# Two chunk transposes moved to DMA, two split products made whole, and an earlier start of a state-space and expert kernel

## The chip, the cores and the metric

The kernel runs on one core of a Trainium2 chip. Its engines are TensorE (PE, with weight loads PEld), VectorE (DVE), ScalarE (ACT), GpSimd (POOL) and SyncE (SP, which only issues transfers here). The metric is the device time of one execution in microseconds; a time is the median of several runs. All times below are microseconds unless another unit stands there.

## The reference

`x` has 2048 tokens of 1024 values in bfloat16. The result is `x + A(layernorm(x)) + B(layernorm(x))`.

```
# A: a diagonal state space, 1024 complex states
Lam_bar = exp(dt * Lam);  B_bar = ((Lam_bar - 1) / Lam)[:, None] * Bmat
Bu = einsum("bld,pd->blp", x, B_bar)
h = Lam_bar * h + Bu[:, t, :]                    # over 2048 steps
y = 2 * einsum("blp,dp->bld", h, Cmat).real + x * Dskip
# B: the two tokens of highest r = x @ w_r go through a gated expert
idx = argsort(-r)[:2];  g = silu(x_sel @ w_gate);  u = x_sel @ w_up
x + scatter(idx, ((g * u) @ w_down) * sigmoid(r[idx]))
```

## The kernel before

The tokens are cut into 16 chunks of 128 and 8 groups (frames) of two chunks. A chunk goes through these stages:

- Its rows are loaded (`x.c`, tile `xt`), the layernorm's sums are taken (`bs.c`, `bn.c` on VectorE for chunks 0 to 5, `sum.c`, `sq.c` on ScalarE for the others), ScalarE makes the reciprocal deviation (`rstd.c`, two instructions on `lv` and `rstd_all`), and `apply.c` writes the normalized chunk `xn`.
- The chunk is transposed into `xnT`. Chunks 0 to 5 go through TensorE and a PSUM bank (`Tpe.c`, L367; chunk 0 in two halves `TpeA` and `Tpe.0`, L373), and ScalarE or VectorE copies the bank out (`xnT.c`, L378, L380, L383). The others go by a transposing DMA that SP issues (`T.c`, L386).
- `Bu.f.j` (L652) multiplies group f by one of eight column blocks of B, real and imaginary part, 16 products of 256 columns in one PSUM bank out of three. For five pairs (f, j) in `HALVES` the two chunks are multiplied apart, as `Bh.f.j` and `Bu.f.j` of 16 products of 128 columns each, so that the first can run before the second chunk is there. ScalarE copies the bank out (`u.f.j`, L658).
- VectorE turns `u` into the frame of a real recurrence (`TI.c`, tiles `m` and `v`), scans it (`SC.c`, tile `gf`, L722) and turns it back (`TO.c`, tiles `hT` and `m`, L763 to L765); GpSimd makes the carry from chunk to chunk. `Y.c.q` (L839) multiplies `hT` by the loaded C, `ADD.c` adds and `out.c` stores. Chunks 0 and 1 are turned and scanned in two halves.

The tables that `TI`, `SC` and `TO` need are made at the start. The parameters are loaded into `prow`, TensorE transposes them (`pP`), VectorE makes `frq` and the angles `th` (`turns`, `whole`, `angle`), ScalarE the sine `sf`, two first columns (`first`, tile `scr`) and the cosine `cf`, after loading the table of sine functions (`trig`) and before loading the one with logarithm and exponential again (`log`). `sq1` squares the cosine on VectorE, `inv` inverts it on ScalarE, `rc`, `R0`, `R`, `tan` follow on VectorE, and `kappa` (seven small GpSimd instructions on `scr`, L565 to L571) makes the factor that `ts`, `E2c` and `E2s` need.

The order of all work is the list `ORDER`: each task there issues its instructions on its own engine, and an engine runs them in that order. A transfer holds one of eight completion counters in turn, and its issue waits for the transfer that held that counter before.

The first transfers stand ahead of the list: SP loads chunk 0 in two halves (L164), ScalarE loads one parameter row, chunks 1 and 2 (L173) and three more parameter rows (L169), and then its function table (L176). `warm` tasks are products that nobody reads; three of them (`prime`, L282) have 512 columns.

Of the kernel before, what the change touches and what calls it, by code (L numbers as in the profile page):

```python
# [25 lines left out]
B.0.0 xa x.0 x.1 B.0.1 bs.0 bn.0 nmean.0 start.0 x.3 x.2 rstd.0 bs.1 bn.1 applyA apply.0 bs.2 rstd.1 apply.1 nmr1.0 warm.0 warm.1 warm.2 warm.3 warm.4  # L26
warm.5 warm.6 warm.7 warm.8 warm.9 warm.10 warm.11 warm.12 B.1.1 warm.13 warm.14 warm.15 warm.16 warm.17 warm.18 warm.19 warm.20 warm.21 warm.22 TpeA
Tpe.0 xnT0 bn.2 bs.3 bn.3 xnT.0 pP.0 Tpe.1 xnT.1 Bh.0.0 Bu.0.0 B.1.0 B.3.0 nmean.1 nmr1.1 nmean.2 rstd.2 nmr1.2 apply.2 Tpe.2 nmr.2 rstd.3 nmean.3
pcol.0 rsum Bh.0.1 Bu.0.1 nmr.1 u.0.0 wr B.2.0 dt x.5 apply.3 Tpe.3 xnT.2 Bh.1.1 Bh.1.0 B.2.1 frq rad turns whole angle abs trig den x.4 xnT.3 Bu.1.0
Bu.1.1 B.3.1 u.0.1 sin bs.5 bn.5 first Bh.1.2 Bu.1.2 bs.4 x.6 B.4.1 cos u.1.0 u.1.1 Bu.1.3 log bn.4 nmr.3 nmr1.3 sq1.0 rstd.4 apply.4 inv.0 sq1.1 rc.0  # L30
R0.0 Bu.0.2 B.7.0 B.4.0 nmean.5 R.0 Tpe.4 u.1.2 Bu.0.3 rstd.5 apply.5 nmean.4 B.5.0 nmr.5 nmr1.5 u.1.3 Bu.0.4 inv.1 tan.0 u.0.2 Tpe.5 Bu.1.4 rc.1
tan.1 B.5.1 cs ntan.0 nmr1.4 kappa sum.6 R0.1 u.0.3 Bu.1.5 ts.0.0 ts.1.0 B.6.1 TI.0.0 nmean.6 R.1 E2c.0 x.7 u.0.4 B.6.0 B.7.1 C.0.0 cin.0.0 SC.0.0.0
ends xr.0 C.0.1 ntan.1 sq.6 u.1.4 x.8 Bu.0.5 Bu.0.6 u.1.5 xnT.4 u.0.5 Bu.0.7 Bu.1.6 sum.7 xnT.5 u.0.6 nmean.7 sq.7 Bu.1.7 nmr.0 ts.0.1 u.0.7 Bu.2.0
u.1.6 u.1.7 E2c.1 nmr.4 E2n.1 SC.0.0.1 cw.0.0 gb.0.0.0 cy.0.0 cin.1.0 gb.0.0.1 rstd.7 Bu.2.1 ts.1.1 E2s.1 TI.1.0 TI.0.4 TI.1.4 E2n.0 cin.0.4 C.1.0
SC.0.4.0 SC.0.4.1 u.2.0 u.2.1 nmr.7 E2s.0 apply.7 T.7 xr.1 Bu.2.2 Bu.2.3 Bu.2.4 u.2.2 Bu.2.5 gb.0.4.0 cw.0.4 gb.0.4.1 SC.1.0.0 cy.0.4 cin.1.4 nmr1.7
TO.0.0 u.2.3 cw.1.0 SC.1.0.1 cy.1.0 Drow rstd.6 nmr.6 apply.6 T.6 x.9 x.10 u.2.4 SC.1.4.0 cw.1.4 Bu.2.6 Bu.2.7 xnT.6 gb.1.0.1 seed.0.0 TO.0.4 seed.0.1
gb.1.0.0 Y.0.0 gb.1.4.0 u.2.5 u.2.6 SC.1.4.1 xs.0 xr.2 gb.1.4.1 xs.1 cin.2.0 cy.1.4 TI.2.0 TI.3.0 C.1.1 Y.0.1 Y.0.2 u.2.7 TO.1.0 sum.9 nmean.9
seed.1.0 xnT.7 Bu.3.0 Bu.3.1 u.3.0 Bu.3.2 sq.9 rstd.9 nmr1.9 nmr.9 TO.1.4 u.3.1 Y.1.0 Y.1.1 xm.0 cin.2.4 x.12 ADD.0.0 seed.1.1 out.0.0 apply.9 Y.0.3
SC.2.0.0 SC.2.0.1 Bu.3.3 cw.2.0 Bu.3.4 xm.1 T.9 u.3.2 Bu.3.5 ADD.1.0 cy.2.0 TI.4.0 gb.2.0.0 sum.8 out.1.0 ADD.0.1 gb.2.0.1 xs.2 nmean.8 cin.3.0 Y.1.2
Y.1.3 w.0 xm.2 sum.12 seed.2.0 nmean.12 xnT.9 SC.3.0.0 r.0 sq.8 rstd.8 nmr.8 cw.3.0 apply.8 x.11 u.3.3 u.3.4 u.3.5 SC.3.0.1 cy.3.0 cin.4.0 gb.3.0.1  # L40
TO.2.0 T.8 gb.3.0.0 ADD.1.1 out.1.1 SC.4.0.0 SC.4.0.1 out.0.1 cw.4.0 cy.4.0 cin.5.0 sq.12 Bu.3.6 Bu.3.7 rstd.12 xnT.8 Y.2.0 Bu.4.0 nmr.12 xr.3 nmr1.6
sum.11 seed.2.1 nmean.11 TO.3.0 Y.2.1 nmr1.12 ADD.2.0 u.3.6 seed.3.0 u.3.7 Y.2.2 Y.2.3 xs.3 xm.3 apply.12 Bu.4.1 gb.4.0.0 T.12 out.2.0 gb.4.0.1
seed.3.1 Y.3.0 TI.5.0 u.4.0 u.4.1 ADD.2.1 sum.10 SC.5.0.0 cw.5.0 xr.4 Bu.4.2 xs.4 Y.3.1 gb.5.0.0 u.4.2 sq.11 TO.4.0 SC.5.0.1 xr.5 Y.3.2 Y.3.3 seed.4.0
out.2.1 Bu.4.3 Bu.4.4 w.1 cy.5.0 w.2 nmean.10 sq.10 rstd.10 nmr.10 apply.10 T.10 gb.5.0.1 ADD.3.0 ADD.3.1 xnT.10 Y.4.0 Bu.4.5 rstd.11 u.4.3 Y.4.1
seed.4.1 w.3 xm.4 Bu.4.6 cin.6.0 TI.6.0 SC.6.0.0 SC.6.0.1 cw.6.0 nmr.11 ADD.4.0 apply.11 xr.6 Y.4.2 x.14 u.4.4 TO.5.0 u.4.5 gb.6.0.0 u.4.6 gb.6.0.1
nmr1.10 Bu.4.7 T.11 xnT.11 x.13 seed.5.0 seed.5.1 cy.6.0 out.3.1 TI.7.0 Y.4.3 ADD.4.1 w.4 Y.5.0 xs.5 Y.5.1 out.3.0 sum.13 u.4.7 Bu.5.0 Bu.5.1 out.4.0
xm.5 nmean.13 sq.13 xs.6 seed.6.0 cin.7.0 SC.7.0.0 SC.7.0.1 rstd.13 nmr.13 x.15 ADD.5.0 TO.6.0 gb.7.0.0 Y.5.2 Y.5.3 xr.7 Bu.5.2 gb.7.0.1 xm.6 apply.13
seed.6.1 u.5.0 Y.6.0 Y.6.1 sum.14 Bu.5.3 TI.8.0 ADD.5.1 nmean.14 sq.14 out.4.1 rstd.14 nmr.14 w.5 u.5.1 Bu.5.4 Y.6.2 out.5.0 cw.7.0 xr.9 cy.7.0
cin.8.0 SC.8.0.0 SC.8.0.1 TI.9.0 TO.7.0 u.5.2 Bu.5.5 xnT.12 cw.8.0 cy.8.0 cin.9.0 seed.7.0 Y.6.3 T.13 sum.15 xnT.13 nmean.15 sq.15 nmr1.11 ADD.6.0
# [12 lines left out]
gb.14.0.1 w.38 w.39 xr.14 seed.14.0 w.40 w.41 out.11.1 TO.14.0 guT.3 Y.13.1 Y.13.2 Y.13.3 gT.3 ADD.13.0 seed.14.1 SC.15.4.0 SC.15.4.1 ADD.13.1 mm.6
mm.7 Y.14.0 SC.15.0.0 SC.15.0.1 xr.15 rows row_.3 row_.1 row_.2 Y.14.1 Y.14.2 Y.14.3 SC.15.6.0 SC.15.6.1 ymb hotY.14.1 hotY.14.0 xs.14 seed.15.0 xm.14
TO.15.0 ADD.14.0 seed.15.1 ADD.14.1 seed.15.2 out.12.1 TO.15.4 TO.15.6 out.12.0 hotY.15.0 Y.15.0 Y.15.1 Y.15.2 Y.15.3 Y.15.4 Y.15.5 Y.15.6 Y.15.7
hotY.15.2 hotY.15.1 Y.15.8 xs.15 xm.15 ADD.15.0 ADD.15.1 ADD.15.2 out.13.0 out.13.1 fix out.14.0 out.14.1 out.15.0 out.15.1 out.15.2
# [39 lines left out]
def kernel(  # L105
# [135 lines left out]

    add(("xa",), "none", 2.85, lambda: None, key=-1)
    for c in range(NCH):
        if c < 3:
            add(("x", c), "none", (3.35, 0.6, 0.6)[c], lambda: None, [("x", c - 1)] if c else [], key=c, takes=[("xt", c, [("apply", c)])])
        elif c == 3:
            add(("x", c), "SP", 0.45, lambda c=c: load_x(c), key=-89.85, takes=[("xt", c, [("apply", c)])], mb=0.28, lag=0.2)
# [917 lines left out]
```

## Time and profile before

| | |
|---|---|
| median of 3 runs (lowest, highest) | 255.83 (255.74, 256.82) |
| profiled execution: time, span | 255.56, 253.8 |
| PE busy | 246.7 (97%) |
| DVE busy | 239.8 (94%) |
| ACT, POOL busy | 175.5 (69%), 93.1 (37%) |
| chain that ended last | PE 65%, DVE 25%, POOL 3%, ACT 2% |

The span runs from the first to the last instruction; 1.76 of the profiled time lies around it. TensorE and VectorE are both busy nearly all the time, so the chain that ended last passes from one to the other: it is mostly on VectorE, ScalarE and GpSimd up to 83 and on TensorE from there on.

### The profile page before, as it was taken

The page shows a single profiled execution, that of the slowest core. Times are in us where ns is not written, and L with a number is a line of the kernel's source. Part 1 is how long each engine was busy: PE and PEld are TensorE (multiplying, and loading weights), DVE is VectorE, ACT ScalarE, POOL GpSimd, SP SyncE. Part 2 cuts the span into 40 slices and gives each one's busy share as a digit, 9 for nine tenths or more (in the row PEclk, how much of TensorE's full clock was granted, in tenths as well). Part 3 has the DMA queues.
Part 4 walks back from the last instruction along what each step waited for, and adds up shares of the span by engine and source line. Part 5 has one row for each costly group of instructions (what it writes and reads, how often), then busy time and mean ns, then how long its engine had stood idle before and what let it go on. Part 6 is the DMA issues. An engine that isn't in the chain of part 4 may idle for free.

```text
span 253.8 us, 5220 instructions
## 1 busy us (share of the span) xinstructions
PE 246.7 (97%) x2052; PEld 167.0 (66%) x2052; DVE 239.8 (94%) x312; ACT 175.5 (69%) x302; POOL 93.1 (37%) x130
## 2 busy tenths in 40 slices
...
GB/s 196 225 228 184 191 254 274 148 134 198 99 159 45 83 89 242 40 256 228 120 89 1 105 166 69 76 3 155 321 340 381 361 316 388 384 250 357 23 68 83
DMA packets 66277, 46.50 MB, mean 183 GB/s; under 512 B 45828, under 2 KB 52362, under 8 KB 66252
## 3 DMA queue, kind: packets, MB, share of 16 engines
...
q0 software_dynamic: 112, 0.27, 0.3%
q14 instruction: 9, 0.07, 0.1%
...
## 4 chain that ended last, share of the span: by engine, by line
PE 65%; DVE 25%; POOL 3%; ACT 2%; DMA 1%; issue 1%; ACTq 0%; DVEq 0%; POOLq 0%
PE pY L839 38%; PE pB L652 22%; DVE gf L722 7%; PE pG L1043 3%; DVE v L703 3%; DVE m L702 2%; DVE m L764 1%; DVE hT L763 1%; DVE ot L850 1%; DVE hT L765 1%; PE pD L1083 1%; DMA xt<-in_A_x_dram 1%; DVE st L294 1%; DVE ts L585 1%; DVE E2c L591 1%
## 5 line engine op out<-in xcount | busy, mean ns | idle before, releaser
L652 PE MATMUL pB<-xnT,BT 128*128 128x256 bf16 (+1 forms) x1104 | 116.9, 265 | 0.6 <-ACT xnT L378 0.3
L839 PE MATMUL pY<-CT,hT 128*128 128x512 bf16 (+1 forms) x528 | 115.7, 373 | 0.2 <-DVE hT L765 0.2
L652 PEld LDWEIGHTS <-BT 128*128 128x128 bf16 x1104 | 100.9, 98 | 16.4 <-issue 1.7
L839 PEld LDWEIGHTS <-hT 128*128 128x128 bf16 x528 | 50.8, 98 | 55.4 <-issue 2.1
L738 POOL TENSOR_TENSOR cw<-gf,tL 128x16 f32<-128x16 f32 (+1 forms) x34 | 41.1, 1210 | 110.8 <-DVE gf L722 101.3
L722 DVE TENSOR_TENSOR_SCAN gf<-R,v 128x1040 f32<-128x1040 f32 (+1 forms) x34 | 68.8, 2056 | 0.5
L658 ACT CAST u<-pB 128x512 bf16<-128x512 f32 x64 | 35.7, 577 | 18.3 <-PE pB L652 15.5
L815 ACT ACTIVATE pY<-xr,nmr_all,rstd_all 128x512 f32<-128x512 bf16 (+1 forms) x33 | 24.9, 763 | 29.2 <-DVE ot L850 24.7
L728 ACT CAST gb<-gf 128x1024 bf16<-128x1024 f32 (+1 forms) x34 | 31.4, 941 | 8.0 <-DVE gf L722 8.0
L850 DVE TENSOR_TENSOR ot<-pY,ot 128x512 bf16<-128x512 f32 (+1 forms) x33 | 21.5, 663 | 3.3 <-PE pY L839 2.1
L765 DVE TENSOR_TENSOR hT<-hT,m 128x2048 bf16<-128x2048 bf16 (+2 forms) x20 | 20.2, 1012 | 0.7
L703 DVE TENSOR_TENSOR v<-u,m 128x2048 bf16<-128x2048 bf16 (+2 forms) x20 | 20.2, 1012 | 0.7
L702 DVE TENSOR_TENSOR m<-u,E1t 128x2048 bf16<-128x2048 bf16 (+2 forms) x20 | 20.1, 1005 | 0.6
L764 DVE TENSOR_TENSOR m<-gb,E2s 128x2048 bf16<-128x2048 bf16 (+2 forms) x20 | 20.3, 1014 | 0.0
L824 ACT ACTIVATE ot<-xr,nmr_all,rstd_all 128x1024 bf16<-128x1024 bf16 x16 | 19.8, 1237 | 0.6 <-DMA out_dram<-ot 0.5
L763 DVE TENSOR_TENSOR hT<-gb,E2c 128x2048 bf16<-128x2048 bf16 (+2 forms) x20 | 20.0, 1000 | 0.0
L753 POOL CAST v<-cy 128x16 bf16<-128x16 f32 (+1 forms) x17 | 12.7, 747 | 1.0
L754 POOL TENSOR_TENSOR v<-cy,v 128x16 bf16<-128x16 f32 (+1 forms) x17 | 12.5, 738 | 1.4
L334 ACT ACTIVATE xn<-xt,nmr_all,rstd_all 128x1024 bf16<-128x1024 bf16 x10 | 12.4, 1237 | 0.2
L309 ACT ACTIVATE xn<-xt,nmean_all 128x1024 bf16<-128x1024 bf16 x10 | 11.5, 1150 | 0.2
L829 DVE TENSOR_TENSOR ot<-ot,Drow 128x1024 bf16<-128x1024 bf16 x16 | 10.9, 680 | 0.0
L303 ACT ACTIVATE xn<-xt 128x1024 bf16<-128x1024 bf16 x10 | 10.5, 1050 | 0.0
...
## 6 DMA issues: line engine op xcount, KB each, us to landing
...
```

The costliest lines, as they stand in the source:

```text
L652: nc.tensor.matmul(out=pB[:, ri, ts_], lhsT=BT[ri][j][:, k, :], rhs=xnT_frame(f)[:, k, ts_], start=(k == 0), stop=(k == DT - 1))
L658: nc.scalar.copy(out=u_tiles[f][:, :, j, :], in_=pB_tiles.pop((f, j))[:])
L702: nc.vector.tensor_tensor(out=m[:, :, js, :], in0=u[:, ::-1], in1=E1t[:, :, js, :], op=ALU.mult)
L703: nc.vector.tensor_add(out=rot, in0=u, in1=m[:, :, js, :])
L722: nc.vector.tensor_tensor_scan(out=flat(gf), data0=flat(R[:, js, :]), data1=flat(v[:, ri, js, :]), initial=0.0, op0=ALU.mult, op1=ALU.add)
L728: nc.scalar.copy(out=gb_tiles[c][:, ri, js, :], in_=gf_tiles[c, js.start, ri][:, :, 2:])
L738: nc.gpsimd.tensor_tensor(out=cw_tiles[c, js.start][:, ri, :, 0:n], in0=g.unsqueeze(1).to_broadcast([128, 2, n]), in1=tL[:, ri, :, js], op ...
L764: nc.vector.tensor_tensor(out=m[:, :, js, :], in0=g[:, ::-1], in1=both(E2s, js), op=ALU.mult)
L765: nc.vector.tensor_add(out=rot, in0=rot, in1=m[:, :, js, :])
L815: nc.scalar.activation(out=pY[:, 0:d_.stop - d_.start], in_=y_tiles["xr", c][:, d_], func=ACT.Identity, bias=nmr_all[:, c:c + 1], scale=rs ...
L839: nc.tensor.matmul(out=pY, lhsT=h_tiles[c][:, ri, j, :], rhs=CT[ri][h][:, j, d0:d0 + w], start=False, stop=end, skip_group_check=True)
L850: nc.vector.tensor_add(out=ot, in0=y_tiles.pop(("pY", c, dh))[:, 0:d_.stop - d_.start], in1=ot)
```

## The change

- Chunks 4 and 5 are transposed by DMA (`PE_T` from 6 to 4): `T.4` and `T.5` on SP replace `Tpe.4`, `Tpe.5` and their copies.
- `HALVES` loses (1, 1) and (1, 2).
- ScalarE's queue issues four early transfers, three parameter rows and then chunk 1. Chunk 2 is issued by SP, the fourth parameter row by GpSimd.
- The halves of chunk 0 are transposed into two PSUM banks, chunk 1 into a bank of the ring for products; 15 `warm` tasks stand in place of 23.
- `ORDER` is another list.

```
-start and first two lines of ORDER: B.0.0 xa x.0 x.1 B.0.1 bs.0 bn.0 nmean.0 start.0 x.3 x.2 rstd.0 ...
+start.0 warm.0 ... warm.6 xa bs.0 x.0 bn.0 rstd.0 warm.7 x.1 bs.1 bn.1 warm.8 x.3 x.2 ... B.0.0 B.0.1 rstd.1 applyA apply.0 B.1.0 pP.0 TpeA
...
-    load_param(nc.scalar, 0)
-    for c in (1, 2):
-        nc.scalar.dma_start(out=xt_tiles[c][:], in_=x2[c * T:(c + 1) * T, :])
-    for i in range(1, 4):
+    for i in range(3):
         load_param(nc.scalar, i)
+    nc.scalar.dma_start(out=xt_tiles[1][:], in_=x2[T:2 * T, :])
     nc.scalar.preload_act_table_set("natural_log_exp_and_others")
...
     nc.vector.tensor_copy(out=tt[:], in_=t_i[:])
+    load_param(nc.gpsimd, 3)
...
-        pT_tiles[c] = psum.tile([128, DT, 128], BF16, name="pT", tag="misc" if odd else "T")
+        pT_tiles[c] = psum.tile([128, DT, 128], BF16, name="pT", tag="B" if c == 1 else "misc" if odd else "T", bufs=3 if c == 1 else 1)
...
-        if h == 0:
-            pT_tiles[0] = psum.tile([128, DT, 128], BF16, name="pT", tag="T")
+        pT_tiles[0, h] = psum.tile([128, DT // 2, 128], BF16, name="pT", tag="misc" if h else "T")
...
-    NWARM = 23
+    NWARM = 15
...
-    PE_T = 6
+    PE_T = 4
...
-    HALVES = ((0, 0), (0, 1), (1, 0), (1, 1), (1, 2))
+    HALVES = ((0, 0), (0, 1), (1, 0))
```

The new order moves instructions in many places; two matter below. The first is the head of SP's queue, before; `BT_0` is the first column block of B, with its real and imaginary part, and the first row is chunk 0:

```order
L164 DMA xt<-in_A_x_dram 128x512 x2
L234 DMA_TRANSPOSE BT_0_116<-in_A_B_re_dram 128x8x128
L234 DMA_TRANSPOSE BT_0_124<-in_A_B_im_dram 128x8x128
L230 DMA xt<-in_A_x_dram 128x1024
L234 DMA_TRANSPOSE BT_1_125<-in_A_B_im_dram 128x8x128
```

And the same head now:

```order
L164 DMA xt<-in_A_x_dram 128x512 x2
L229 DMA xt<-in_A_x_dram 128x1024 x2
L233 DMA_TRANSPOSE BT_0_114<-in_A_B_re_dram 128x8x128
L233 DMA_TRANSPOSE BT_0_122<-in_A_B_im_dram 128x8x128
L233 DMA_TRANSPOSE BT_1_115<-in_A_B_re_dram 128x8x128
```

Chunks 3 and 2 now stand ahead of the first two blocks of B. Further on, `T.4` stands between the blocks 5 and 6 of B and `T.5` behind block 7.

The second place is ScalarE around the sine tables, before; `xnT` rows copy a transposed chunk, `u` rows a finished product, `sf` is the sine, the two `scr` rows are `first`, `cf` is the cosine, and the table loads are `trig` and `log`:

```order
L483 ACTIVATE rad<-scr 128x8
L505 ACT_TABLE_LOAD
L380 COPY xnT<-pT 128x8x128
L658 CAST u<-pB 128x2x256
L517 ACTIVATE sf<-th 128x1024
L512 ACTIVATE scr<-th 128x8
L513 ACTIVATE scr<-cf,halfpi 128x8
L520 ACTIVATE cf<-cf,halfpi 128x1024
L658 CAST u<-pB 128x2x256 x2
L508 ACT_TABLE_LOAD
```

And now:

```order
L378 COPY xnT<-pT 128x8x128 x2
L481 ACTIVATE rad<-scr 128x8
L503 ACT_TABLE_LOAD
L510 ACTIVATE scr<-th 128x8
L511 ACTIVATE scr<-cf,halfpi 128x8
L656 CAST u<-pB 128x2x256
L515 ACTIVATE sf<-th 128x1024
L656 CAST u<-pB 128x2x256 x2
L518 ACTIVATE cf<-cf,halfpi 128x1024
L506 ACT_TABLE_LOAD
```

Both copies of transposed chunks now stand ahead of `rad` and the table, `first` ahead of the sine, and three copies of products between `first` and the cosine; before, one stood ahead of the sine and two behind the cosine.

## Rows read from the trace of the kernel before

**Rows 1.** ScalarE's timeline at the start: start, duration, instruction, [idle before <-releaser]

```profile
0.73 0.59 ACTq L169 DMA_DIRECT2D prow<-in_A_Lambda_re_dram  x1
...
2.63 0.30 ACTq L169 DMA_DIRECT2D prow<-in_A_log_dt_dram  x1
...
4.86 1.28 ACT L176 ACT_TABLE_LOAD   x1 [4.86 <-DMA xt<-in_A_x_dram]
```

**Rows 2.** Chain that ended last, one piece: start, duration, what (chunk 1's load)

```profile
1.36 3.17 DMA xt<-in_A_x_dram
```

**Rows 3.** VectorE's timeline from the first chunks to the first hT

```profile
4.78 1.23 DVE L294 BATCH_NORM_STATS2 st<-xt 128x6 f32<-128x512 bf16 x2
6.05 0.21 DVE L297 BATCH_NORM_AGGREGATE mv<-st 128x2 f32<-128x12 f32 x1
...
6.71 0.74 DVE L330 TENSOR_SCALAR xn<-xt,mv,rstd_all 128x512 bf16<-128x512 bf16 x2 [0.46 <-ACT rstd_all L263]
...
10.86 0.21 DVE L297 BATCH_NORM_AGGREGATE mv<-st 128x2 f32<-128x12 f32 x1
...
12.63 1.23 DVE L493 TENSOR_TENSOR th<-frq,tt 128x1024 f32<-128x1024 f32 x1
...
15.88 0.69 DVE L501 TENSOR_SCALAR cf<-th 128x1024 int32<-128x1024 int32 x1
...
20.20 0.64 DVE L524 TENSOR_TENSOR th<-cf 128x512 f32<-128x512 f32 x1
...
22.58 0.69 DVE L534 TENSOR_TENSOR gf<-gf,cf 128x512 f32<-128x512 f32 x1
...
29.48 1.31 DVE L585 TENSOR_TENSOR ts<-sf,scr 128x512 f32<-128x512 f32 x2 [0.46 <-POOL scr L571]
...
53.77 0.70 DVE L765 TENSOR_TENSOR hT<-hT,m 128x1024 bf16<-128x1024 bf16 x1
```

**Rows 4.** TensorE's timeline up to 84

```profile
3.04 1.49 PE L282 MATMUL prime<-ident 128*128 128x512 bf16 x3
4.32 1.86 PE L399 MATMUL warm<-ident 128*128 128x128 bf16 x24
...
11.54 0.62 PE L367 MATMUL pT<-ident,xn 128*128 128x128 bf16 x8
11.99 1.95 PE L652 MATMUL pB<-xnT,BT 128*128 128x128 bf16 x32
...
27.47 26.36 PE L652 MATMUL pB<-xnT,BT 128*128 128x256 bf16 x240
53.67 5.36 PE L839 MATMUL pY<-CT,hT 128*128 128x512 bf16 x24
...
83.26 1.90 PE L839 MATMUL pY<-CT,hT 128*128 128x512 bf16 x8 [0.23 <-DVE hT L765]
```

**Rows 5.** ScalarE's timeline around the sine tables

```profile
16.01 1.07 ACT L517 ACTIVATE sf<-th 128x1024 f32<-128x1024 f32 x1
...
17.41 1.15 ACT L520 ACTIVATE cf<-cf,halfpi 128x1024 f32<-128x1024 f32 x1
18.47 1.05 ACT L658 CAST u<-pB 128x512 bf16<-128x512 f32 x2
19.54 1.28 ACT L508 ACT_TABLE_LOAD   x1
...
21.27 0.62 ACT L530 ACTIVATE gf<-th 128x512 f32<-128x512 f32 x1
```

**Rows 6.** GpSimd's timeline, first and last instruction of kappa

```profile
24.77 0.50 POOL L565 TENSOR_TENSOR scr<-scr,rad 128x16 f32<-128x16 f32 x1
...
29.17 0.28 POOL L571 TENSOR_SCALAR scr<-scr 128x16 f32<-128x16 f32 x1
```

**Rows 7.** DMA issues: transfer, queue, kind, count, median time to landing

```profile
BT<-in_A_B_re_dram SPq DMA_TRANSPOSE x8, 4.3
```

**Rows 8.** SP's timeline, two blocks of B: start, time to issue

```profile
22.62 2.67 SPq L234 DMA_TRANSPOSE BT<-in_A_B_im_dram  x2
```

More of the change, by code (lines that the diff above doesn't have):

```diff
@@ L25 @@
 ORDER = """
[L26 to L49, printed above, removed]
@@ L62 @@
[L62 to L65, printed above, removed]
+start.0 warm.0 warm.1 warm.2 warm.3 warm.4 warm.5 warm.6 xa bs.0 x.0 bn.0 rstd.0 warm.7 x.1 bs.1 bn.1 warm.8 x.3 x.2 warm.9 warm.10 warm.11 warm.12
@@ new lines @@
+warm.13 warm.14 B.0.0 B.0.1 rstd.1 applyA apply.0 B.1.0 pP.0 TpeA Tpe.0 bs.3 apply.1 Tpe.1 xnT0 xnT.0 Bh.0.0 xnT.1 Bu.0.0 nmean.0 B.1.1 nmr1.0 nmr.0
+bn.3 rstd.3 B.2.0 bs.2 nmean.1 bn.2 rstd.2 nmean.3 nmr1.3 pcol.0 dt wr apply.3 Tpe.3 apply.2 Tpe.2 Bh.0.1 Bu.0.1 u.0.0 x.4 frq rsum x.5 xnT.3 xnT.2
+Bh.1.0 Bu.1.0 Bu.1.1 B.2.1 turns whole angle abs rad trig first u.0.1 Bu.0.2 bs.4 bs.5 sin u.1.0 u.1.1 den nmr1.1 nmean.2 nmr1.2 bn.5 cos bn.4 log
+nmean.4 sq1.0 sq1.1 inv.0 rc.0 R0.0 B.3.0 nmean.5 Bu.1.2 B.3.1 Bu.1.3 u.0.2 rstd.4 apply.4 u.1.2 nmr.1 inv.1 nmr.2 u.1.3 R.0 x.6 tan.0 B.4.0 rstd.5
@@ new lines @@
+Bu.0.3 ntan.0 nmr1.4 u.0.3 rc.1 tan.1 cs ntan.1 B.4.1 Bu.1.4 B.5.0 B.5.1 nmr.4 kappa ts.0.1 u.1.4 ts.1.0 TI.0.0 apply.5 Bu.0.4 Bu.0.5 T.4 Bu.1.5 B.6.0
+sum.6 B.6.1 u.0.4 Bu.0.6 u.0.5 E2c.1 B.7.0 nmean.6 nmr.3 sq.6 Bu.1.6 u.1.5 ts.0.0 B.7.1 Bu.0.7 R0.1 T.5 rstd.6 nmr1.6 E2c.0 R.1 x.7 cin.0.0 E2n.0
+u.0.6 xnT.4 E2n.1 xnT.5 TI.1.0 u.1.6 nmr.6 u.0.7 SC.0.0.0 SC.0.0.1 xr.0 sum.7 nmr.5 nmean.7 Bu.1.7 Bu.2.0 sq.7 rstd.7 C.1.0 ends C.0.0 u.1.7 Bu.2.1
+Bu.2.2 gb.0.0.1 gb.0.0.0 TI.0.4 cin.0.4 ts.1.1 TI.1.4 SC.0.4.0 u.2.0 u.2.1 SC.0.4.1 gb.0.4.0 gb.0.4.1 cw.0.0 cy.0.0 cin.1.0 nmr.7 C.0.1 Bu.2.3 u.2.2
```

71 lines of the change are left out of this document (45 added, 26 removed).

## The prediction

> **What bounds the kernel now.** I read the page's busy shares first: TensorE 97% and VectorE 94% of a span of 253.8, in an execution of 255.56. Two engines that full bound each other, so a part of the sum must name which one waits. The timelines answer that. TensorE runs without a gap from the transpose at 11.54 to the first output product at 53.67 and on to 83.26, where it waits 0.23 for `hT` of VectorE [rows 4]. VectorE has its last `hT` half for the first output products done at 53.77 + 0.70 = 54.47 [rows 3], 0.8 after those products began: they read the first half of the states first, so nothing was lost. VectorE is thus as late as it may be, with nothing to spare, and its own chain starts at the first layernorms and runs through the sine tables of ScalarE and `kappa` of GpSimd [rows 3, 5, 6]. An edit that frees TensorE alone gains only what VectorE can follow.
>
> **The start.** ScalarE's table load began at 4.86, after a sixth issue had waited for chunk 1 to land [rows 1, 2], and VectorE waited 0.46 for the deviation it delayed, to apply chunk 0 at 6.71 [rows 3]. With four issues and no wait the table is in long before. But in VectorE's order chunk 1's statistics stand ahead of that apply; they took from 4.78 to 6.05 + 0.21 = 6.26 [rows 3]. So the gain is at most 6.71 - 6.26 = 0.45. Chunk 1 is now ScalarE's fourth issue: 0.73 + 0.59, then two short ones like the one of 0.30 [rows 1], so about 2.05 in place of 1.36. It landed 3.17 after its issue [rows 2]; the same again is 5.2, and since less stands in its queue I take 5.0. VectorE then starts these statistics 0.2 later than at 4.78, and applies chunk 0 at about 6.45: a gain of 0.25. The other end is the 4.3 that a block of B of the same 256 KB took to land [rows 7]: 2.05 + 4.3 = 6.35, apply at 7.85, a loss of 1.1.
>
> The Trainium skill bears on this place (DMA: Bandwidth & Descriptors, section Issuing engines are not separate DMA queues): transfers of all issuing engines interleave on the same 16 DMA engines, so that another queue saves issuing time alone. By it chunk 1 shares with chunk 3, which SP now issues early, lands at 5.2 or later, and the gain falls to 0.05; were queues apart it would be the full 0.45. Chunk 1's 3.17, beside other loads, is on the rule's side, but no row shows a queue alone.
>
> **TensorE.** A transpose of a chunk takes 11.99 - 11.54 = 0.45 from start to start [rows 4]; two go: 0.9. A whole product takes 16 x (53.67 - 27.47) / 240 = 1.75; the same in two halves took 1.95 at most, with the modelled end of the last [rows 4]. So each of two costs 0 to 0.2 less; I take 0.05 each. Together 1.0 less. Against that, chunks 3 and 2 are now transposed ahead of the second column block, behind both chunks' statistics: these ended at 10.86 + 0.21 [rows 3], then two casts and apply 3, together 0.8, so 11.9 less the 0.25 gained, or 0.1 later than 11.54. And `Bu.0.3` takes the PSUM bank whose copy `u.0.2` now stands behind the inverse: by the ScalarE times below that copy ends at 23.75 where TensorE would be at 23.4, 0.35. TensorE could be at the first output products at 53.67 - 1.0 + 0.1 + 0.35 = 53.1.
>
> **The table chain, without the 0.25.** VectorE's work up to the angles is the same set, so `th` starts at 12.63 again and the absolute value ends at 15.88 + 0.69 = 16.57 [rows 3]. ScalarE's `first` waits for that and now stands ahead of the sine, and three product copies stand between it and the cosine. Sine and `first` took 17.41 - 16.01 = 1.40, the cosine 18.47 - 17.41 = 1.06, two copies 1.05 [rows 5]. So the cosine ends at 16.6 + 1.40 + 3 x 0.53 + 1.06 = 20.65, where it ended at 18.47. The squares, at 20.20 before [rows 3], wait for it; that alone is 0.5. The table load takes 1.3 and the inverse 22.58 - 21.27 = 1.3 [rows 3, 5]: `rc.0` comes at 23.25 in place of 22.58. Before it VectorE had also applied chunk 4, about 0.5, which now comes later, so VectorE is 1.1 behind. Next on ScalarE are `u.0.2` and the deviation of chunk 4, 0.5 each; with 0.8 for two GpSimd instructions `kappa` starts at 25.0, takes 29.17 + 0.28 - 24.77 = 4.7 [rows 6] and ends at 29.7. VectorE's `ts`, which waited 0.46 for it and began at 29.48 [rows 3], begins at 29.7 with two instructions still to do that were done before (apply 5 and a part of R, 1.2 together). From there to the last `hT` it needed 54.47 - 29.48 = 25.0; these two come on top and one half scan falls behind it, which I set equal: 54.7. Less 0.25: 54.45.
>
> **The sum.** Of the two halves of chunk 0's states the first is now turned back last, and the first output product reads it: TensorE, ready at 53.1, starts at 54.45, 0.8 later than at 53.67. Behind this point its work is the same, and the new order leaves VectorE as little room as the old one, so I leave its later waits as they were. The execution takes 255.56 + 0.8 = 256.35. The median of the runs lies 0.27 above the profiled execution; by it the same sum is 256.6, and I forecast 256.5.
>
> Cost nothing: the two ScalarE copies (2 us that nobody waited for after 30), the separate PSUM banks (the copy no longer waits for VectorE's, but the products still need both), the parameter row on GpSimd (TensorE's `pP` now stands ahead of chunk 0's transposes and waits for it; GpSimd issues it near 1.6, and a landing after 4.3 [rows 7] is before 6.45; later than that it delays all), fewer `warm` tasks.
>
> **Rivals.**
>
> 1. VectorE follows, and TensorE's time counts. For it: 1.0 less work is certain, and ScalarE loses two copies. Against it: the cosine cannot start before the copies ahead of it. TensorE at 53.1 in place of 53.67: 255.0, by the median 255.25, and 254.9 if the bank's 0.35 goes too. Chance 0.22.
>
> 2. Slower: chunk 1 lands late. Everything on VectorE stands behind its statistics, and VectorE is the bound up to the output products, so each 0.1 is paid in full. It decides from a landing of about 5.5, where 0.8 has become 1.3; at 6.35 the time is 256.35 + 1.35 = 257.7, by the median 258.0. For it: issued 0.7 later, beside chunks 3 and 2; against it: chunk 1 is alone in its queue. Chance 0.20.
>
> 3. SP stands still at `T.4` until chunk 4 is applied, near 25.1, with the blocks 6 and 7 of B behind. At 1.33 an issue [rows 8] the last is issued at 25.1 + 4 x 1.33 = 30.4 and lands 4.3 later, 34.7 [rows 7]; TensorE wants it ten products before 53.1, at 35.6. A stop 0.9 longer delays TensorE, one 2.2 longer the whole. With 3 longer it is 257.4. Chance 0.06.
>
> 4. TensorE's clock. The three 512-column products took (4.32 - 3.04) / 3 = 0.43 each [rows 4], the 1.2 GHz level; later 128 columns take 0.061 at most, the 2.4 GHz one. Eight `warm` tasks less leave TensorE idle from about 5.2 to 6.45, and little used up to the first products. At the low level 32 products cost 0.107 in place of about 0.056 each, 1.6 in all; TensorE is then at 54.7 and the end 0.3 to 0.8 later: 257. Chance 0.07. The Trainium skill has this as a rule (TensorE: Matmul & The Clock Gate, section What's actually happening): activity releases the throttle and an idle stretch brings it back; the granted clock on the page is full in all 40 slices, so no row of before shows a fall.
>
> **How the numbers follow.** The forecast has 0.45. About 0.5% (1.3) is what a measurement of this kernel tells from no change: faster means under 254.55, slower over 257.1. Faster: half of rival 1 with a luckier start, 0.12. Slower: nearly all of rivals 2 and 3, half of 4, a little of the forecast, 0.31. The same: the rest, 0.57. The range runs from rival 1's early end, 254.6, to rival 2's price, 258.0; the forecast alone has 255.9 to 257.1.
>
> **What would show it.** On VectorE, chunk 0's apply near 6.45 and chunk 1's statistics ending just before; idle time ahead of the squares (0.5 or more), ahead of `rc.0` (about 1.0) and ahead of `ts` (0.5 to 1.0, released by GpSimd); on ScalarE the cosine ending near 20.4; on TensorE a wait of about 1.3 for `hT` at the first output products, near 54.4. If TensorE starts them near 53.1 without a wait, the chain was mis-sized and rival 1 holds. If VectorE waits for a load ahead of chunk 1's statistics until after 5.5, it is rival 2.

## The result and the profile after

| | before | after |
|---|---|---|
| median (lowest, highest), 10 runs each | 255.86 (255.34, 256.82) | 257.83 (256.83, 258.90) |
| profiled execution: time, span | 255.56, 253.8 | 257.90, 256.1 |
| PE busy, DVE busy | 246.7, 239.8 | 245.6, 239.8 |
| first output product | 53.67 | 55.75 |
| from there to the end of the span | 200.1 | 200.4 |

The ratio of the changed kernel's time to that of the kernel before is 1.0069, 95% interval [1.0046, 1.0092]: 1.8 slower. The forecast was 256.5 with a range of 254.6 to 258.0. The traces differ by 2.3, and 2.08 of it has arisen when TensorE starts the first output products; what follows takes the same time in both within 0.3. So the place to look is the first 56.

ScalarE's timeline at the start (start, duration, instruction), where the third row is chunk 1's load:

```profile
0.74 0.59 ACTq L169 DMA_DIRECT2D prow<-in_A_Lambda_re_dram  x1
...
2.03 0.39 ACTq L173 DMA_DIRECT2D xt<-in_A_x_dram  x1
2.45 1.28 ACT L174 ACT_TABLE_LOAD   x1 [2.45 <-issue]
```

The chain of waits holds that load:

```profile
2.03 4.63 DMA xt<-in_A_x_dram
```

The table is in 2.4 earlier than before [rows 1], as forecast. But chunk 1 took 4.63 from its issue to landing, at 6.66, where it took 3.17 [rows 2]. VectorE's timeline (in brackets: idle time before, and who ended it) shows what that does:

```profile
3.04 1.29 DVE L293 BATCH_NORM_STATS2 st<-xt 128x6 f32<-128x512 bf16 x2 [0.44 <-DMA xt<-in_A_x_dram]
...
6.69 1.29 DVE L293 BATCH_NORM_STATS2 st<-xt 128x6 f32<-128x512 bf16 x2 [2.12 <-DMA xt<-in_A_x_dram]
...
8.13 0.68 DVE L329 TENSOR_SCALAR xn<-xt,mv,rstd_all 128x512 bf16<-128x512 bf16 x2
...
14.09 1.22 DVE L491 TENSOR_TENSOR th<-frq,tt 128x1024 f32<-128x1024 f32 x1
...
22.39 1.29 DVE L522 TENSOR_TENSOR th<-cf 128x512 f32<-128x512 f32 x2 [0.66 <-ACT cf L518]
25.00 0.69 DVE L532 TENSOR_TENSOR gf<-gf,cf 128x512 f32<-128x512 f32 x1 [1.31 <-ACT gf L529]
...
31.31 1.29 DVE L583 TENSOR_TENSOR ts<-sf,scr 128x512 f32<-128x512 f32 x2 [0.63 <-POOL scr L569]
...
55.00 0.69 DVE L763 TENSOR_TENSOR hT<-hT,m 128x1024 bf16<-128x1024 bf16 x1
```

The first two rows are the statistics of chunk 0 and of chunk 1. VectorE stood idle for 2.12 and applied chunk 0 at 8.13, 1.42 later than at 6.71 [rows 3]. The angles are 1.46 later, `rc.0` 2.42, the last half of `hT` 1.22. TensorE's timeline:

```profile
5.10 0.18 PE L465 MATMUL pP<-ident,prow 32*128 32x32 bf16 x1 [0.21 <-DMA prow<-in_B_w_r_dram]
8.55 1.03 PE L371 MATMUL pT<-ident,xn 128*128 128x128 bf16 x8 [3.27 <-DVE xn L329]
9.93 1.03 PE L366 MATMUL pT<-ident,xn 128*128 128x128 bf16 x8 [0.34 <-DVE xn L322]
10.75 3.62 PE L650 MATMUL pB<-xnT,BT 128*128 128x128 bf16 x32
14.16 1.20 PE L366 MATMUL pT<-ident,xn 128*128 128x128 bf16 x16
15.20 40.42 PE L650 MATMUL pB<-xnT,BT 128*128 128x128 bf16 x400
55.75 4.49 PE L837 MATMUL pY<-CT,hT 128*128 128x512 bf16 x19
```

TensorE idled 3.27 before chunk 0 came. Then 32 products of 128 columns took 3.62, where 1.95 had done [rows 4]. Busy times and granted clock by stretch (the last three figures are the clock, 1.00 being full speed, the busy share of the DMA engines, and GB/s) say why:

```profile
5.00:10.00 5.00, 1.29 (x10) 0.94 (x11) 3.28 (x8) 1.22 (x4) 0.62 (x3) 0.76 1.10 227
10.00:15.00 5.00, 5.00 (x53) 5.00 (x54) 4.80 (x15) 2.60 (x8) 1.46 (x5) 0.55 0.92 225
...
9.00:11.00 2.00, 1.66 (x17) 1.40 (x15) 1.97 (x6) 0.59 (x2) 0.00 (x0) 0.50 1.01 215
...
13.00:15.00 2.00, 2.00 (x26) 2.00 (x25) 1.97 (x7) 0.69 (x3) 0.77 (x2) 0.64 1.02 257
```

The granted clock fell to half (0.50), the 1.2 GHz level, within the idle stretch and rose again before 15; in the kernel before it reads full in every slice. The DMA engines are busy nearly throughout (1.10 and 0.92). ScalarE's timeline around the sine tables:

```profile
19.09 1.05 ACT L515 ACTIVATE sf<-th 128x1024 f32<-128x1024 f32 x1
20.05 1.26 ACT L656 CAST u<-pB 128x512 bf16<-128x512 f32 x2
21.20 1.15 ACT L518 ACTIVATE cf<-cf,halfpi 128x1024 f32<-128x1024 f32 x1
22.37 1.28 ACT L506 ACT_TABLE_LOAD   x1
```

The cosine ends at 22.35, 3.8 later than before [rows 5]. The two copies ahead of it wait for TensorE's products. The chain of waits goes through them:

```profile
10.96 3.41 PE pB L650 x32
14.37 0.99 PE pT L366 x16
15.37 5.33 PE pB L650 x80
20.72 0.58 ACT u L656
21.31 1.05 ACT cf L518
```

So TensorE's slow clock reaches VectorE's tables.

### The profile page after: what moved, and what is told of

Its sections match the earlier page's. It is cut to its first block, busy times and chain, and to the rows that moved or that the text cites. A ratio compares the mean times of both kernels' runs of the same rounds, so it can differ in the third digit from the quotient of the medians.

```text
span 256.1 us, 5068 instructions
## 1 busy us (share of the span) xinstructions
PE 245.6 (96%) x1969; PEld 166.5 (65%) x1988; DVE 239.8 (94%) x312; ACT 173.5 (68%) x300; POOL 86.3 (34%) x131
## 4 chain that ended last, share of the span: by engine, by line
PE 75%; DVE 15%; DMA 3%; ACT 2%; POOL 2%; issue 2%; ACTq 0%; SPq 0%; DVEq 0%
PE pY L837 38%; PE pB L650 31%; PE pG L1041 3%; DVE gf L720 2%; DMA xt<-in_A_x_dram 2%; DVE v L701 1%; DVE hT L763 1%; DVE m L700 1%; DVE hT L761 1%; DVE m L762 1%; DVE ts L583 1%; DVE ot L848 1%; DVE gb L713 1%; DVE E2c L589 1%; DVE E2s L589 1%
## 5 line engine op out<-in xcount | busy, mean ns | idle before, releaser
L837 PE MATMUL pY<-CT,hT 128*128 128x512 bf16 (+1 forms) x509 | 112.4, 372 | 2.0 <-issue 0.6
L650 PEld LDWEIGHTS <-BT 128*128 128x128 bf16 x1072 | 102.2, 99 | 15.2 <-PE pG L1041 0.4
L736 POOL TENSOR_TENSOR cw<-gf,tL 128x16 f32<-128x16 f32 (+1 forms) x34 | 35.0, 1028 | 116.6 <-DVE gf L720 115.7
L751 POOL CAST v<-cy 128x16 bf16<-128x16 f32 (+1 forms) x17 | 13.5, 792 | 1.1
L744 POOL TENSOR_TENSOR cy<-cw 128x16 f32<-128x16 f32 (+1 forms) x17 | 11.1, 652 | 1.3
L752 POOL TENSOR_TENSOR v<-cy,v 128x16 bf16<-128x16 f32 (+1 forms) x17 | 10.2, 599 | 1.4
```

Source lines behind the costliest of these rows:

```text
L650: nc.tensor.matmul(out=pB[:, ri, ts_], lhsT=BT[ri][j][:, k, :], rhs=xnT_frame(f)[:, k, ts_], start=(k == 0), stop=(k == DT - 1))
L736: nc.gpsimd.tensor_tensor(out=cw_tiles[c, js.start][:, ri, :, 0:n], in0=g.unsqueeze(1).to_broadcast([128, 2, n]), in1=tL[:, ri, :, js], op ...
L837: nc.tensor.matmul(out=pY, lhsT=h_tiles[c][:, ri, j, :], rhs=CT[ri][h][:, j, d0:d0 + w], start=False, stop=end, skip_group_check=True)
```

## The experiments

Theory: VectorE's chain bounds up to the first output products, and chunk 1's late landing is most of its delay. Rivals: the lost clock; the order around the sine tables; the moved transposes. Medians, with the ratio to runs of the kernel before on the same chip:

| kernel | time | ratio, interval | chunk 0 applied | first output product |
|---|---|---|---|---|
| `x1_first` | 255.93 | 0.9994 [0.9967, 1.0021] | 6.77 | 53.83 |
| `warm_on` | 257.44 | 1.0051 [1.0024, 1.0078] | 8.13 | 55.18 |
| `sine_first` | 257.23 | 1.0051 [1.0022, 1.0079] | 8.61 | 55.91 |
| `three` | 255.56 | 0.9981 [0.9949, 1.0014] | 6.83 | 53.36 |
| `x23_behind` | 257.71 | 1.0070 [1.0047, 1.0094] | 9.16 | 57.00 |
| `best` | 256.09 | 1.0009 [0.9987, 1.0030] | 6.64 | 54.46 |
| `before_dma45` | 256.35 | 1.0019 [0.9998, 1.0040] | 6.65 | 57.18 |
| `before_early` | 258.63 | 1.0112 [1.0077, 1.0147] | 8.91 | 56.21 |
| `x1_sp` | 255.33 | 0.9994 [0.9979, 1.0008] | 5.75 | 52.81 |
| `best2` | 255.19 | 0.9981 [0.9967, 0.9995] | 6.11 | 52.41 |
| `x1_pe45` | 257.47 | 1.0062 [1.0046, 1.0077] | 6.77 | 55.05 |
| `before_x1sp` | 255.58 | 1.0000 [0.9975, 1.0024] | 5.81 | 55.07 |

The last two columns are of the one profiled execution, which lies well above the median in `before_dma45` (258.34, by 2.0), `x23_behind` (259.15, by 1.4), `before_x1sp` (256.74, by 1.2), `sine_first` (258.38, by 1.2) and `best` (257.02, by 0.9).

**Chunk 1 first: `x1_first`.**

```diff
+    nc.scalar.dma_start(out=xt_tiles[1][:], in_=x2[T:2 * T, :])
     for i in range(3):
         load_param(nc.scalar, i)
-    nc.scalar.dma_start(out=xt_tiles[1][:], in_=x2[T:2 * T, :])
```

> The changed kernel with chunk 1's transfer as the first issue of ScalarE's queue, ahead of the three parameter rows. Theory (chunk 1's late landing at 6.66 delays all of VectorE, and VectorE bounds the time up to the first output products): chunk 1 is issued near 0.75 and lands by 5.0, the first half of chunk 0 is applied by 6.7 in place of 8.13, the first output products start 1.1 to 1.5 earlier than at 55.75, and the time falls by as much, to 256.3 to 256.8. Rival (TensorE's lost clock sets the end, or the table chain absorbs the earlier start): apply comes earlier but the first output products move by less than 0.5 and the time stays above 257.3.

VectorE and TensorE of this kernel:

```profile
3.93 1.29 DVE L293 BATCH_NORM_STATS2 st<-xt 128x6 f32<-128x512 bf16 x2 [1.33 <-DMA xt<-in_A_x_dram]
...
6.77 0.68 DVE L329 TENSOR_SCALAR xn<-xt,mv,rstd_all 128x512 bf16<-128x512 bf16 x2
...
23.07 0.69 DVE L532 TENSOR_TENSOR gf<-gf,cf 128x512 f32<-128x512 f32 x1 [1.31 <-ACT gf L529]
...
29.39 1.29 DVE L583 TENSOR_TENSOR ts<-sf,scr 128x512 f32<-128x512 f32 x2 [0.63 <-POOL scr L569]
...
53.08 0.69 DVE L763 TENSOR_TENSOR hT<-hT,m 128x1024 bf16<-128x1024 bf16 x1
```

```profile
12.82 40.60 PE L650 MATMUL pB<-xnT,BT 128*128 128x128 bf16 x400
53.83 5.35 PE L837 MATMUL pY<-CT,hT 128*128 128x512 bf16 x23 [0.41 <-DVE hT L763]
```

Chunk 0 is applied 1.36 earlier than in the changed kernel, the first output product 1.92 earlier, and the time falls by 1.9: all of the loss, by moving one line. The theory's 1.1 to 1.5 was too small, because the granted clock stayed at full speed here too (1.00 from 5 to 15). The first row shows the price: chunk 0, on another engine's queue, now comes 0.9 later (its statistics begin at 3.93, in the changed kernel at 3.04).

**The clock: `warm_on`.** `hold` is a task list of the products of `warm`:

```diff
-B.1.0 pP.0 TpeA
+B.1.0 pP.0 hold.0 hold.1 ... hold.25 TpeA
```

> The changed kernel with 52 products of 128 columns that nobody reads, behind the transpose of the parameters on TensorE, so that it isn't idle from 5.1 to about 8.3. Theory (TensorE waits for VectorE at the first output products anyway): the granted clock stays at full speed through 7.6 to 14.5, the first products of chunk 0 take half the time, but the first output products start within 0.3 of 55.75 and the time stays at 257.5 to 258.2. Rival (the lost clock is the loss): 256.0 to 257.0.

```profile
10.00:15.00 5.00, 4.22 (x71) 3.92 (x72) 4.79 (x15) 3.55 (x9) 1.02 (x5) 1.00 1.08 212
```

```profile
8.13 0.68 DVE L330 TENSOR_SCALAR xn<-xt,mv,rstd_all 128x512 bf16<-128x512 bf16 x2
...
24.43 0.69 DVE L536 TENSOR_TENSOR gf<-gf,cf 128x512 f32<-128x512 f32 x1 [1.30 <-ACT gf L533]
```

With the clock full and chunk 0 applied at the very same 8.13, `rc.0` comes 0.57 earlier and the first output product too (55.18). The theory said at most 0.3, since TensorE would only wait; it left out that ScalarE's copies of TensorE's products stand ahead of the cosine. The medians are 0.39 apart with intervals that overlap; the 0.57 is shown by the traces alone. The clock is the lesser part. TensorE's own delay stood close behind this one: in the changed kernel its last product before that point ends at 15.20 + 40.42 = 55.62, and the last half of `hT` at 55.69.

**The order around the sine tables: `sine_first`.**

```diff
-trig first u.0.1 Bu.0.2 bs.4 bs.5 sin u.1.0 u.1.1 den nmr1.1 nmean.2 nmr1.2 bn.5 cos bn.4 log
+trig u.0.1 sin first Bu.0.2 bs.4 bs.5 den nmr1.1 nmean.2 nmr1.2 bn.5 cos u.1.0 u.1.1 bn.4 log
```

> The changed kernel with ScalarE's order around the sine tables as before: sine, then the two first columns, then the cosine, with one product copy ahead and two behind. Theory (the cosine behind three copies is the other part of VectorE's delay): the cosine ends near 20.2 in place of 22.35, the squares start without a wait, rc.0 starts near 23.7 in place of 25.0, the first output products 0.5 to 1.1 earlier; time 256.8 to 257.4. Rival (the table chain has slack, all of the loss is the late chunk): within 0.3 of the changed kernel, 257.5 to 258.1.

Here chunk 1 happened to land 0.48 later still (2.03 + 5.11 in the chain, apply at 8.61). Counted from the apply, `rc.0` comes 0.28 earlier than in the changed kernel and the first output product 0.32. The medians differ by 0.6, the ratios by 0.0018, inside their intervals. This run can't size the order by itself: counted from the apply, TensorE's long run of products also starts 0.24 earlier (15.44 in place of 15.20), and its 32 first products took 3.49 in place of 3.62: the granted clock rose at nearly the same moment (0.56 and 0.55 from 10 to 15) although chunk 0 came later. The next run sizes it with the clock at 1.00.

**All three: `three`,** the edits above together, with 12 of the 26 tasks.

> All three at once: chunk 1 first on ScalarE's queue, 24 more products that nobody reads on TensorE before chunk 0 comes, and ScalarE's order around the sine tables as before. Theory (VectorE's chain bounds; the two parts on it add): the first output products 1.6 to 2.6 earlier than at 55.75, near 53.6, and the time 255.2 to 256.2, level with the kernel before. Rival (TensorE's work bounds once VectorE is ahead, 1.0 less than before): 254.8 to 255.2. Rival (the loss lies behind the first output products): above 257.

```profile
22.59 0.69 DVE L536 TENSOR_TENSOR gf<-gf,cf 128x512 f32<-128x512 f32 x1 [1.02 <-ACT gf L533]
```

```profile
12.88 40.42 PE L654 MATMUL pB<-xnT,BT 128*128 128x128 bf16 x400
53.36 5.35 PE L841 MATMUL pY<-CT,hT 128*128 128x512 bf16 x23
```

53.36 without a wait, and 255.56: level with the kernel before, as the theory had it. Against `x1_first` the first output product gains 0.47. `rc.0` comes at 22.59 in place of 23.07, although chunk 0 is applied 0.06 later, and TensorE's long run of products starts no earlier (12.88 and 12.82). So the order around the sine tables costs about 0.5 on VectorE, the lower end of what was expected of `sine_first`; the medians, 0.37 apart, don't separate it from noise.

**Why chunk 1 was late: `x23_behind`.** SP's head is the first block of B, then chunks 3 and 2:

```diff
-x.3 x.2 ... B.0.0 B.0.1
+B.0.0 x.3 x.2 B.0.1
```

> The changed kernel with the first transposing load of B issued ahead of chunks 3 and 2 on SP instead of behind them; chunk 1 stays the fourth issue of ScalarE's queue, at 2.03. It tells why chunk 1 landed at 6.66. Theory (the transfers share the same DMA engines, and chunks 3 and 2 on SP took chunk 1's share): chunk 1 lands 3.2 to 3.6 after its issue, at 5.2 to 5.6, the first half of chunk 0 is applied by 7.2, time 256.0 to 256.7. Rival (it is the place in its own queue, or one DMA engine that is behind whatever SP issues): chunk 1 lands at 6.4 or later, apply at 7.9 to 8.3, time 257.3 to 258.1.

```profile
2.03 5.66 DMA xt<-in_A_x_dram
```

The rival's time and landing came (257.71, 7.69; the apply, 9.16, is later still), and the theory fell in this form: chunks 3 and 2 are not what chunk 1 needs to be ahead of, since with a block of B issued at 1.66 in their place the time is the same. What the two have in common is 256 KB issued before chunk 1. But this trace, of the slowest of its twelve runs, isn't a plain case of waiting in line. The trace has sixteen completion marks for each load: fourteen of chunk 1's stand by 5.73, 3.7 after its issue, the last two at 7.04 and 7.70, and the block of B issued ahead of it landed only at 7.9. In the changed kernel twelve of chunk 1's stand by 6.09 and the last at 6.67. Why single marks come late stays open. The next run puts chunk 1 ahead.

**Chunk 1 behind chunk 0 on SP: `x1_sp`.**

```diff
-    nc.scalar.dma_start(out=xt_tiles[1][:], in_=x2[T:2 * T, :])
+    nc.sync.dma_start(out=xt_tiles[1][:], in_=x2[T:2 * T, :])
```

> The changed kernel with chunk 1 issued by SP right behind the two halves of chunk 0, ahead of chunks 3 and 2, and not by ScalarE. Its issue comes at about 1.66 in place of 2.03, and all of x now stands in one queue in the order in which it is wanted. Theory (the DMA engines are busy from 2 on and move what was issued first; chunk 1 came last of the first four chunks): chunk 1 lands by 5.2, 0.5 to 1.5 before chunks 3 and 2, the second half of chunk 0 stays near 3.5, apply by 6.7, time 255.4 to 256.2. Rival (one or two DMA engines lag whatever stands ahead, as with the first block of B ahead of chunks 3 and 2): chunk 1 lands at 6 or later, apply at 7.5 or later, time above 257.

```profile
1.67 0.43 SPq L173 DMA_DIRECT2D xt<-in_A_x_dram  x1
```

```profile
2.91 1.29 DVE L293 BATCH_NORM_STATS2 st<-xt 128x6 f32<-128x512 bf16 x2 [0.32 <-DMA xt<-in_A_x_dram]
...
4.36 1.23 DVE L293 BATCH_NORM_STATS2 st<-xt 128x6 f32<-128x512 bf16 x2
...
5.75 0.68 DVE L329 TENSOR_SCALAR xn<-xt,mv,rstd_all 128x512 bf16<-128x512 bf16 x2
```

Issued 0.36 earlier and with only chunk 0 and parameter rows of 2 KB ahead, chunk 1 landed 2.4 after its issue, in place of 4.63, and VectorE didn't wait for it. Against `x1_first` the apply moves by 1.02 and the first output product by 1.02 as well: up to there each 0.1 at the start is paid, or won, in full. The times show less of it: the medians, 255.93 and 255.33, are 0.6 apart and of different chips, and the two ratios are equal.

**The early transfers in the kernel before: `before_early`,** with that part of the change alone, **and `before_x1sp`,** the same with chunk 1 on SP behind chunk 0 and chunk 2 ahead of chunk 3.

```diff
-    load_param(nc.scalar, 0)
-    for c in (1, 2):
-        nc.scalar.dma_start(out=xt_tiles[c][:], in_=x2[c * T:(c + 1) * T, :])
-    for i in range(1, 4):
+    for i in range(3):
         load_param(nc.scalar, i)
+    nc.scalar.dma_start(out=xt_tiles[1][:], in_=x2[T:2 * T, :])    # before_x1sp: nc.sync
...
+    load_param(nc.gpsimd, 3)
...
-B.0.0 xa x.0 x.1 B.0.1 ... x.3 x.2
+xa x.0 x.1 x.3 x.2 B.0.0 B.0.1
```

> The kernel before with the other part of the change: ScalarE's queue issues three parameter rows and then chunk 1, GpSimd the fourth row, SP chunks 3 and 2 ahead of the first block of B; all else as before. Theory (this part alone makes the loss): chunk 1 lands at 6.4 to 7, the first half of chunk 0 is applied at 7.9 to 8.4 in place of 6.71, the last half of hT ends 1.2 to 1.7 later than at 54.47, time 257.0 to 257.7. Rival (the loss comes from the new order of the instructions, which can't cover the late chunk): 255.8 to 256.5.

> The kernel before with the early transfers of the change, but chunk 1 issued by SP right behind chunk 0, then chunks 2 and 3, then the blocks of B; ScalarE issues three parameter rows and its table, GpSimd the fourth row. All else, the order too, as before. Theory (the early transfers are worth what they do to chunk 1's landing, in either order of the instructions): chunk 1 lands near 4.1, the first half of chunk 0 is applied at 5.6 to 6.0 in place of 6.71, the last half of hT ends 0.6 to 1.0 earlier than at 54.47; time 254.6 to 255.1. Rival (the old order can't use an earlier start, since TensorE or a later load sets it): 255.3 to 255.8.

`before_early` is 2.85 slower, more than expected and more than the whole change: chunk 1's load took 5.41, and the granted clock averaged 0.69 from 10 to 15. In `before_x1sp` chunk 0 was applied at 5.81, as expected, but the time is that of the kernel before. TensorE of it:

```profile
10.58 0.62 PE L366 MATMUL pT<-ident,xn 128*128 128x128 bf16 x8
13.39 1.96 PE L651 MATMUL pB<-xnT,BT 128*128 128x128 bf16 x32 [2.19 <-DMA BT<-in_A_B_re_dram]
```

The second column block of B, which SP issued at 7.50, came only near 13.4, and TensorE lost there what it had won. The new order transposes chunks 3 and 2 before it wants that block; in this execution the old one couldn't use the early start. Three of the twelve runs took 254.91 to 254.96, inside the expected 254.6 to 255.1, so the wait may not come in each; that is not shown, since the one trace is of a slower run.

**The moved transposes: `before_dma45`,** `T.4` and `T.5` behind `B.5.1` and two split products made whole, in the kernel before, **and `x1_pe45`,** `x1_first` with `Tpe.4` and `Tpe.5` in their place again.

```diff
-    PE_T = 6
+    PE_T = 4
-    HALVES = ((0, 0), (0, 1), (1, 0), (1, 1), (1, 2))
+    HALVES = ((0, 0), (0, 1), (1, 0))
```

> The kernel before with one part of the change: chunks 4 and 5 transposed by DMA and two split products made whole, all else as before. It takes 1.0 of TensorE's work away ahead of the first output products. Theory (VectorE bounds up to them): TensorE comes to them 0.7 to 1.0 earlier than at 53.67 and waits there or a little later for hT, whose last half still ends near 54.5; time 255.5 to 256.0, no change. Rival (TensorE bounds): 254.8 to 255.1. Rival (the two transposes delay the last blocks of B on SP's queue): TensorE waits for them before 40 and the time is above 256.3.

> The kernel with chunk 1 first on ScalarE's queue, and chunks 4 and 5 transposed on TensorE again (0.9 more of its work, two more copies on ScalarE). There TensorE was ready at 53.42 and waited 0.41 for hT. Theory (TensorE and VectorE come to that point nearly together, so that TensorE's 0.9 can gain no more than the rest over the wait): TensorE comes at 54.2 to 54.4 and doesn't wait, time 256.2 to 256.6. Rival (VectorE alone bounds): within 0.2 of 255.93. Rival (TensorE alone bounds): 256.8.

Taking 1.0 of TensorE's work away gained nothing (ratio 1.0019; 256.35 is at the edge of the second rival). It doesn't settle why, nor whether VectorE alone bounded the kernel before, since its trace has a new wait: ScalarE's `sum.6` needs the buffer that `T.4` and `T.5` read.

```profile
29.40 1.06 ACT L303 ACTIVATE xn<-xt 128x1024 bf16<-128x1024 bf16 x1 [2.98 <-DMA xnT<-xn]
```

Putting the transposes back on TensorE cost 1.5, three times the 0.5 expected, for the same reason turned round:

```profile
31.20 1.06 ACT L302 ACTIVATE xn<-xt 128x1024 bf16<-128x1024 bf16 x1 [2.56 <-PE pT L366]
```

ScalarE stands still for the buffer, its copies of products come late, and TensorE waits 0.60 and VectorE 0.96 for a `u`. The first output product comes 1.22 later than in `x1_first`: 0.9 for the two transposes, 0.60 for that wait, 0.12 for a later start of the long run of products, less the 0.41 that TensorE no longer waits for `hT`. The transposes' place is worth more than their 0.9 of TensorE.

**Two combinations: `best`,** `three` (with 10 of the tasks) and SP's head as `x.3 B.0.0 x.2 B.0.1`, **and `best2`,** `x1_sp`, 8 of the tasks, the old order around the sine tables, `pP.0` behind `Tpe.0`, and `TO.0.0` ahead of `TO.0.4`.

> The kernel with the three edits (chunk 1 first on ScalarE's queue, products that nobody reads until chunk 0 comes, the old order around the sine tables) and SP's head as chunk 3, one block of B, chunk 2, the next block of B. In the kernel with the three edits the second half of chunk 0 landed at 4.33 in place of 3.50, beside chunk 1. Theory (VectorE's start still sets the time, and chunk 2 takes its share): chunk 0 is applied 0.3 to 0.7 earlier than at 6.83, time 254.8 to 255.3. Rival (chunk 0 and chunk 1 take the share from each other, chunk 2 has no part in it): apply near 6.8, time 255.4 to 255.9.

> The same, with 16 products that nobody reads before chunk 0 comes, the parameters' transpose behind those of chunk 0, the old order around the sine tables, and the first half of chunk 0's states turned back first. If chunk 1 lands by 5.2: apply near 6.2, TensorE at the first output products near 52.8 without a wait, time 254.6 to 255.2, below both kernels. If chunk 1 lands late: as the changed kernel with that order, 256.8 to 257.4.

`best` is no better (apply 6.64, which is 0.19 earlier and short of the theory's 0.3): TensorE waited for a parameter row of 2 KB that landed at 6.84, 4.72 after its issue, and the granted clock averaged 0.79 from 5 to 10.

```profile
6.97 0.17 PE L468 MATMUL pP<-ident,prow 32*128 32x32 bf16 x1 [1.98 <-DMA prow<-in_A_log_dt_dram]
```

`best2` has that transpose out of the way and TensorE without a wait at the first output product; chunk 1, issued as in `x1_sp`, landed after 3.0 here:

```profile
11.25 1.08 PE L366 MATMUL pT<-ident,xn 128*128 128x128 bf16 x16 [0.57 <-DVE xn L322]
12.16 40.42 PE L653 MATMUL pB<-xnT,BT 128*128 128x128 bf16 x400
52.41 5.34 PE L840 MATMUL pY<-CT,hT 128*128 128x512 bf16 x24
```

255.19 against 255.51 of the kernel before: faster than both kernels, by 0.2% over the one [0.9967, 0.9995] and some 0.9% over the other, by ratios from different chips. It starts the output products 1.26 earlier than before and keeps half of that: from there to the end of its span it takes 200.8 in place of 200.1.

## Why the prediction was right, and where it was wrong

The range held, and the bound (VectorE's chain up to the first output products, TensorE after) held by little. But the loss, 0.7% with an interval from 0.46%, is most likely the "slower" to which I gave 0.31, and the case that came is not the forecast's own: it is rival 2, with rival 4 on top. That rival 2's 258.0 lies so near the 257.83 is luck: it was priced for a landing at 6.35 on a table chain 0.89 too long; the landing was 0.31 later and the clock took 0.57, together 0.88.

- **The bound.** At the first output product TensorE waits 0.41 for `hT` in `x1_first` and 0.34 in `warm_on`. In the changed kernel both come within 0.07 (55.62 and 55.69), and in `three` and `best2` TensorE doesn't wait. So VectorE is the later one by 0.4 at most, and by these traces an earlier VectorE alone would gain no more than that.
- **The start.** The step "chunk 1 lands at 5.0" failed: it landed at 6.66. I had taken the load's duration from an execution in which only chunk 0 and a parameter row were issued before it, and shortened it because less stood in its own queue. Its own queue was not what counted: in `x1_sp` chunk 1 stands third in its queue and takes 2.4. Rival 2 named the condition (5.5) and the price: apply at 7.85 and 258.0 for a landing at 6.35. Measured are 8.13 and 257.83, and `x1_first` and `x1_sp` show that each 0.1 is paid in full up to the first output product.
- The rule of the Trainium skill that I weighed there (DMA: Bandwidth & Descriptors, section Issuing engines are not separate DMA queues) is borne out: in `x1_first` a load on ScalarE's queue delays chunk 0 on SP's by 0.9. I drew too little from it: my 5.2 is the issue at 2.05 plus the old 3.17, so that sharing with chunk 3 had no price of its own.
- **TensorE's clock.** The clock of rival 4 came: half clock, products at nearly double time (3.62 for 32, where 1.95 had done). Its price of 0.3 to 0.8 is measured as 0.57 (`warm_on`), but not only by its path: besides TensorE's own lateness, the copies of products ahead of the cosine made VectorE late. A chance of 0.07 was too low, because it hangs on rival 2: chunk 0's late apply made the idle stretch 3.27 long. The rule of the Trainium skill cited there (TensorE: Matmul & The Clock Gate, section What's actually happening) is borne out by the stretches above.
- **TensorE's work.** The 1.0 held: from the transpose of the next chunk behind the first two to the first output product it took 53.67 - 11.54 = 42.13 before and, where nothing holds TensorE up behind it (`best2`), 52.41 - 11.25 = 41.16, 0.97 less. With the chunks in time (`x1_first`) it comes to the output products at 12.82 + 40.60 = 53.42, where I said 53.1.
- **The table chain.** In the changed kernel the waits ahead of the squares, `rc.0` and `ts` came as listed (0.66, 1.31, 0.63); in `x1_first`, without the late chunk, the one ahead of the squares is missing, and the cosine ends at 20.43, where the sum without the start's gain had 20.65. The term was mis-sized: without the start's gain I had 0.8 + 0.25 = 1.05 at the first output product, and `x1_first`, whose start equals that of before within 0.06, has 53.83 - 53.67 = 0.16. `ts` starts at 29.39 where I had 29.7, and from there to the last `hT` it takes 24.4 where I had 25.0: two thirds of the error lie in the stretch where I had set two instructions equal to one half scan. The 0.16 still has about 0.5 for the new order in it (`three`).
- **The two errors together.** 1.92 for the late chunk with the clock (1.35 by the difference of 1.92 and 0.57 is the chunk itself, close to the apply's 1.36) and 0.16 for all else make the 2.08 at the first output product. The forecast had 0.8: a chain 0.9 too long hid part of a chunk put 1.7 too early and of a clock left out.
- **Costed at nothing.** The copies of chunks 4 and 5 on ScalarE are perhaps not nothing: with them and the transposes back (`x1_pe45`) the time is 1.5 longer, but in its trace 0.9 is the transposes and 0.60 a wait for ScalarE, which had itself waited 2.56 for their buffer, and no run takes the copies alone. Nor does one test the separate PSUM banks. Rival 3 (SP standing still at `T.4`) didn't come: TensorE ran without a gap from 15.20 on. The work behind the first output products took the same time within 0.3, as assumed.
